# Decode attention on one core: the scores of K summed in two halves of 128 rows, the second halved three times

## Chip, cores, metric

One core of a Trainium2 chip (8 NeuronCores; the other seven idle). The metric is the device time of one launch in microseconds (us). The kernel before takes 1251.89 us (median of 3 runs, 1251.55 to 1251.96).

## The reference

Attention with one query row per head: 8 x 32 = 256 heads, 4096 keys, head size 128, bf16. K and V are 268.4 MB each and are used once.

```python
B, H, Sq, Skv, Dh = 8, 32, 1, 4096, 128
scores = jnp.einsum('bhqd,bhkd->bhqk', q, k) * q.shape[-1] ** -0.5
attn = softmax(scores, axis=-1)
return jnp.einsum('bhqk,bhkd->bhqd', attn, v)
```

## The kernel before

Eight heads make a group; there are NT = 32 groups, t = 0 to 31. A group's K is 128 partitions x C = 256 rows x D = 128. VectorE multiplies the rows by the query in place and halves the products by adding (128 -> 64, for the second half of the rows -> 32 columns). PE sums on with an identity matrix into a PSUM bank (8 partial sums for each of 64 rows), and VectorE reads the bank with a reduction. Then come the weights (VectorE, ScalarE) and a loop of 64 multiplies of PE over V. Three buffers serve all loads, in the order K(t+1), V(t), K(t+2), ...

```python
G, SLOTS = 8, 3
UC = 64;  DS = 512 // UC;  NU = C // UC
# ... (cut)
def width_of(t, u):
    return D // 4 if u >= NU // 2 and 0 < t < NT - 3 else D // 2

def product(t, lo, hi):
    kt = loads["k", t]; qb = qbs[t]; part = kt[:, lo:hi, :]
    nc.vector.tensor_tensor(out=part, in0=part, in1=qb[:].to_broadcast([P, hi - lo, D]), op=ALU.mult)
    nc.vector.tensor_tensor(out=part[:, :, 0 : D // 2], in0=part[:, :, 0 : D // 2],
                            in1=part[:, :, D // 2 : D], op=ALU.add)
    if width_of(t, lo // UC) < D // 2:
        nc.vector.tensor_tensor(out=part[:, :, 0 : D // 4], in0=part[:, :, 0 : D // 4],
                                in1=part[:, :, D // 4 : D // 2], op=ALU.add)

def sum_over_d(t, u):
    ps = ps_s.tile([P, UC, DS], F32, name="ps", tag="ps")
    n = width_of(t, u) // DS
    for s in range(n):
        nc.tensor.matmul(ps[:], lhsT=ident[:],
            rhs=kt[:, u * UC : (u + 1) * UC, s * DS : (s + 1) * DS], start=(s == 0), stop=(s == n - 1))
# ... (cut)
# one turn of the loop over t, 0 < t <= NT - 3 (cut to its order):
product(t, 0, 2 * Q); sum_over_d(t, 0); sum_over_d(t, 1)
product(t, 2 * Q, 3 * Q); sum_over_d(t, 2); scores_of(t, 0); scores_of(t, 1)
product(t, 3 * Q, C); sum_over_d(t, 3); scores_of(t, 2)
values_loop(t - 1); load("k", t + 1); load("v", t)
scores_of(t, 3); weights_of(t)
```

## Time and profile before

| quantity | before | where it is read |
|---|---|---|
| time | 1251.89 us | median of runs |
| load queue busy | 99.5% | table of DMA queues |
| VectorE busy / idle before K | 1021.9 us / 139.9 us | busy shares / waits |
| one turn of the loop | 38.7 us | timeline, first product to first product |
| V, K from issue to landing | 25.8 / 28.3 us | DMA issues |

"Busy" is the time in which an engine has at least one instruction under way. The wait that VectorE has just before the first product of a turn shows how much of the turn it does not need. The time from issue to landing, less the 19.35 us that one load of 8.39 MB takes in the steady turn (half of 38.7), shows how much of the load ahead was still to come when it was issued. I call this the **lead** of a load. A buffer is *handed over* when its last reader is done, so that the next load into it can be issued. The lines themselves are in the prediction.

### The profile page before, as it was taken

What the parts mean: (1) busy time and instruction counts of PE and PEld (TensorE: products, weight loads), DVE (VectorE), ACT (ScalarE), POOL (GpSimd) and SP (SyncE); (2) the same over time, 40 slices, a digit from 0 to 9 for tenths busy, and PEclk for the clock granted to TensorE, in tenths of its full rate; (3) what the DMA queues carried; (4) which work ended last, traced back from release to release, by engine and by line L of the source; (5) the groups of instructions that cost most, each with busy time, mean ns of one, the idle gap of its engine ahead of it and who ended that gap; (6) DMA issues with size and microseconds to landing.
All of it is one profiled execution on the core that took longest, in us unless ns stands there. A gap on an engine that the chain in (4) does not pass through costs nothing. (4 is left out here: it accounts for less than half of the span.)

```text
span 1250.2 us, 10842 instructions
## 1 busy us (share of the span) xinstructions
PE 786.8 (63%) x3116; PEld 299.6 (24%) x3116; DVE 1021.9 (82%) x495; ACT 166.1 (13%) x433; POOL 4.5 (0%) x24
## 2 busy tenths in 40 slices
PE   3366567666576655766558665577655776556755
PEld 1122123222232222322223222222222222212222
DVE  7887987878977789777798777987779877798783
ACT  0111011111011110111101111011110111101111
POOL 1000000000000000000000000000000000000000
PEclk9987788777888778877788777887778878779867
DMA  9999999999999999999999999999999999999997
GB/s 405 436 436 435 434 436 432 436 430 428 426 437 436 429 435 434 434 435 436 436 434 432 424 437 437 432 430 428 436 437 434 430 433 434 430 435 421 427 446 329
DMA packets 11432, 537.33 MB, mean 430 GB/s; under 512 B 1808, under 2 KB 2064, under 8 KB 2320
## 3 DMA queue, kind: packets, MB, share of 16 engines
q1 hardware_dynamic: 11072, 536.94, 99.5%
q8 instruction: 15, 0.25, 0.1%
q10 hardware_dynamic: 336, 0.07, 0.0%
q14 instruction: 9, 0.07, 0.0%
HBM read 536.94 MB, written 0.07 MB: 430 GB/s over the span
## 5 line engine op out<-in xcount | busy, mean ns | idle before, releaser
L191 DVE TENSOR_TENSOR kt<-kt,qb 128x8192 bf16<-128x8192 bf16 (+1 forms) x99 | 560.9, 5665 | 146.6 <-DMA kt<-in_k_dram 139.9
L211 PE MATMUL ps<-kt,ident 128*128 128x512 bf16 x800 | 278.4, 511 | 389.9 <-DVE kt L199 299.7
L294 PE MATMUL av<-vt,w 128*32 x1740 | 425.5, 397 | 4.6
L194 DVE TENSOR_TENSOR kt<-kt 128x4096 bf16<-128x4096 bf16 (+1 forms) x99 | 288.8, 2917 | 3.4
L294 PEld LDWEIGHTS av<-vt,w 128*32 x1740 | 173.4, 100 | 262.4 <-issue 119.5
L211 PEld LDWEIGHTS <-ident 128*128 128x128 bf16 x800 | 95.7, 120 | 565.4 <-issue 527.9
L223 DVE TENSOR_REDUCE sc<-ps 128x64 f32<-128x512 f32 x128 | 85.3, 685 | 54.0 <-PE ps L211 54.0
L248 ACT ACTIVATE e<-sc,nmax 128x256 bf16<-128x256 f32 x32 | 16.3, 508 | 706.7 <-DVE nmax L242 706.7
L255 ACT ACTIVATE w<-e,mine 128x256 bf16<-128x256 bf16 x256 | 105.6, 495 | 1.1
L199 DVE TENSOR_TENSOR kt<-kt 128x2048 bf16<-128x2048 bf16 x56 | 68.6, 1225 | 1.9
L351 ACT ACTIVATE comb<-av 32x512 bf16<-32x512 f32 (+1 forms) x32 | 18.8, 586 | 329.0 <-PEq L284 321.4
L280 PE MATMUL av<-vt,w 128*32 128x512 bf16 x116 | 47.2, 499 | 14.6 <-issue 13.1
L371 PE MATMUL op<-comb,pick 32*16 32x128 bf16 (+1 forms) x128 | 12.1, 213 | 20.7 <-ACT comb L351 20.7
L280 PEld LDWEIGHTS av<-vt,w 128*32 128x32 bf16 x116 | 6.9, 100 | 55.2 <-issue 55.2
L177 PE MATMUL qp<-qg,heads 8*128 8x128 bf16 x32 | 7.0, 217 | 16.7 <-ACT qg L175 16.7
L371 PEld LDWEIGHTS <-pick 32*16 32x16 bf16 (+1 forms) x128 | 8.7, 83 | 27.7 <-issue 27.3
L322 PE MATMUL av<-vt,w 128*32 128x512 bf16 x188 | 13.7, 418 | 2.3 <-DMA vt<-in_v_dram 2.3
L235 DVE TENSOR_REDUCE pmax<-sc 128x1 f32<-128x256 f32 x32 | 13.4, 420 | 1.1
L175 ACT ACTIVATE qg<-qh 8x128 bf16<-8x128 f32 x32 | 8.5, 266 | 33.5 <-PE qh L171 33.5
L171 PE MATMUL qh<-q_all,ident 128*8 128x128 bf16 x32 | 7.2, 225 | 8.7 <-DMA q_all<-in_q_dram 8.3
L179 ACT ACTIVATE qb<-qp 128x128 bf16<-128x128 f32 x32 | 8.9, 278 | 9.7 <-PE qp L177 9.7
L237 DVE TENSOR_SCALAR spread<-same,pmax 128x32 f32<-128x32 f32 x32 | 7.7, 242 | 1.1
(31 smaller groups left out, 47.7 us busy)
## 6 DMA issues: line engine op xcount, KB each, us to landing
kt<-in_k_dram SPq DMA_DIRECT2D x4, 4096.0 KB, 24.3
kt<-in_k_dram SPq DMA_DIRECT2D x4, 2048.0 KB, 13.0
vt<-in_v_dram SPq DMA_DIRECT2D x1, 4096.0 KB, 33.9
vt<-in_v_dram SPq DMA_DIRECT2D x1, 2048.0 KB, 38.5
vt<-in_v_dram SPq DMA_DIRECT2D x1, 1024.0 KB, 40.5
vt<-in_v_dram SPq DMA_DIRECT2D x1, 512.0 KB, 41.3
vt<-in_v_dram SPq DMA_DIRECT2D x31, 25.8
kt<-in_k_dram SPq DMA_DIRECT2D x29, 28.3
```

Of the source, the lines that this page charges most:

```text
L191: nc.vector.tensor_tensor(out=part, in0=part, in1=qb[:].to_broadcast([P, hi - lo, D]), op=ALU.mult)
L194: nc.vector.tensor_tensor(out=part[:, :, 0 : D // 2], in0=part[:, :, 0 : D // 2], in1=part[:, :, D // 2 : D], op=ALU.add,)
L199: nc.vector.tensor_tensor(out=part[:, :, 0 : D // 4], in0=part[:, :, 0 : D // 4], in1=part[:, :, D // 4 : D // 2], op=ALU.add,)
L211: nc.tensor.matmul(ps[:], lhsT=ident[:], rhs=kt[:, u * UC : (u + 1) * UC, s * DS : (s + 1) * DS], start=(s == 0), stop=(s == n - 1),)
L223: made = nc.vector.tensor_reduce(out=scs[t][:, u * UC : (u + 1) * UC], in_=sums.pop((t, u))[:], axis=AX.X, op=ALU.add)
L248: nc.scalar.activation(out=e[:], in_=sc[:], func=ACT.Exp, bias=nmax[:, 0:1], scale=scale, accum_out=esums[t // R][:, t % R : t % R + 1],)
L255: nc.scalar.activation(out=w[:, :, g, :], in_=e_g, func=ACT.Copy, scale=mine[:, 0, g : g + 1])
L280: pe.matmul(av, lhsT=wf[:, i * nw : (i + 1) * nw], rhs=vf[:, i * nv : (i + 1) * nv], **how)
L294: pe.matmul(av, lhsT=wf[:, bass.ds(ow + i * nw, nw)], rhs=vf[:, bass.ds(ov + i * nv, nv)], start=False, stop=False,)
L322: nc.tensor.matmul(avs[t][j * AG : (j + 1) * AG, :], lhsT=w[:, i, :, :], rhs=vt[:, c0 : c0 + CB, :], start=(i < TG), stop=(j not in group[ ...
L351: nc.scalar.activation(out=comb[0:n, :, :], in_=av[0:n, :, :], func=ACT.Copy)
L371: nc.tensor.matmul(ops[n][:], lhsT=pick[0:e, m, r, :], rhs=comb[0:e, m, :], start=(r == 0 and m == 0), stop=(r == R - 1 and m == CB - 1 an ...
```

## The change

In the loop turns the second half becomes one product over 128 rows, and each half gets one PSUM bank with four partial sums per row and one read. To keep the PE work of the second half small, it is halved three times (to 16 columns, 4 multiplies). The groups outside the loop keep quarters, and t = 29 keeps a width of 64. The intent is fewer, larger instructions on VectorE and fewer on PE.

```diff
-        return D // 4 if u >= NU // 2 and 0 < t < NT - 3 else D // 2
+        return D // 8 if lo == C // 2 and 0 < t < NT - 3 else D // 2
...
-        if width_of(t, lo // UC) < D // 2:
+        n = D
+        while n > width_of(t, lo):
+            n //= 2
             nc.vector.tensor_tensor(
-                out=part[:, :, 0 : D // 4], ...
+                out=part[:, :, 0:n], in0=part[:, :, 0:n], in1=part[:, :, n : 2 * n], op=ALU.add
             )
...
-        ps = ps_s.tile([P, UC, DS], F32, name="ps", tag="ps")
+        ps = ps_s.tile([P, BANK], F32, name="ps", tag="ps")
+        ds = BANK // (hi - lo)
...
+                sum_over_d(t, 0, HALF)
+                product(t, HALF, C)
+                sum_over_d(t, HALF, C)
+                scores_of(t, 0, HALF)
...
                 values_loop(t - 1)
                 load("k", t + 1)
                 load("v", t)
+                scores_of(t, HALF, C)
```

## The prediction

> **What bounds the kernel now.** I first read the page: the busy shares, the DMA row of the slices, and the table of DMA queues.
>
> ```profile
> PE 786.8 (63%) x3116; PEld 299.6 (24%) x3116; DVE 1021.9 (82%) x495; ACT 166.1 (13%) x433; POOL 4.5 (0%) x24
> ...
> DMA  9999999999999999999999999999999999999997
> GB/s 405 436 436 435 434 436 432 436 430 428 426 437 436 429 435 434 434 435 436 436 434 432 424 437 437 432 430 428 436 437 434 430 433 434 430 435 421 427 446 329
> ...
> q1 hardware_dynamic: 11072, 536.94, 99.5%
> ```
>
> No compute engine is full: VectorE is idle 18% of the span. The load queue is busy 99.5% of it, in every slice, at about 434 GB/s, with 536.94 MB to bring (all of K and V once). That makes the load the suspect, but a busy queue is only the bound if nothing lets it run dry, so next come the waits and one turn of the loop over t (groups of 8 heads; t = 1 to 29 take the loop form).
>
> ```profile
> DVE kt L191 <- DMA kt<-in_k_dram: 139.9, 28, 6.3
> ```
>
> The columns are us in total, times, longest. In 28 turns VectorE stands before the first product and waits for K to land: 139.9 / 28 = 5.0 us each. The timeline of one turn, VectorE and then the load issues:
>
> ```profile
> 586.22 8.69 DVE L191 TENSOR_TENSOR kt<-kt,qb 128x16384 bf16<-128x16384 bf16 x1 [4.86 <-DMA kt<-in_k_dram]
> 594.94 4.43 DVE L194 TENSOR_TENSOR kt<-kt 128x8192 bf16<-128x8192 bf16 x1
> 599.29 4.42 DVE L191 TENSOR_TENSOR kt<-kt,qb 128x8192 bf16<-128x8192 bf16 x1
> 603.74 2.29 DVE L194 TENSOR_TENSOR kt<-kt 128x4096 bf16<-128x4096 bf16 x1
> 606.07 1.22 DVE L199 TENSOR_TENSOR kt<-kt 128x2048 bf16<-128x2048 bf16 x1
> 607.21 1.28 DVE L223 TENSOR_REDUCE sc<-ps 128x64 f32<-128x512 f32 x2
> ...
> 615.24 1.22 DVE L199 TENSOR_TENSOR kt<-kt 128x2048 bf16<-128x2048 bf16 x1
> 616.38 0.68 DVE L223 TENSOR_REDUCE sc<-ps 128x64 f32<-128x512 f32 x1
> 618.41 0.69 DVE L223 TENSOR_REDUCE sc<-ps 128x64 f32<-128x512 f32 x1 [1.35 <-PE ps L211]
> ...
> 624.96 8.69 DVE L191 TENSOR_TENSOR kt<-kt,qb 128x16384 bf16<-128x16384 bf16 x1 [4.88 <-DMA kt<-in_k_dram]
> ```
>
> ```profile
> 596.57 0.33 SPq L158 DMA_DIRECT2D kt<-in_k_dram  x1
> 618.41 0.33 SPq L158 DMA_DIRECT2D vt<-in_v_dram  x1
> ```
>
> A turn lasts 624.96 - 586.22 = 38.74 us and brings two buffers of 128 x 256 x 128 x 2 bytes = 8.39 MB, so 16.78 MB / 38.74 us = 433 GB/s; one buffer takes 19.4 us. The work of VectorE, its wait for PE included, ends 4.88 us before the turn does. There are three buffers. The V load goes into the K buffer just read, so it is issued when the last summing multiply is done (618.41, which is 32.2 us after the turn's start). The K load goes into the V buffer just read, so it is issued after the loop of PE over V (596.57).
>
> ```profile
> vt<-in_v_dram SPq DMA_DIRECT2D x31, 25.8
> kt<-in_k_dram SPq DMA_DIRECT2D x29, 28.3
> ```
>
> From issue to landing, V takes 25.8 us and K 28.3, where the transfer itself takes 19.4. So when a load is issued, 6.4 us (V) or 8.9 us (K) of the load before it are still to come: the queue never runs dry, and the buffers are handed over that much earlier than needed. This margin is the number that decides the case. The chain that ended last agrees: its longest piece is 41.43 us of V loads, after which come under 2 us of PE and ScalarE.
>
> **What the Trainium skill says.** *DMA: Bandwidth & Descriptors*, section "Where 436 GB/s comes from", puts the ceiling into SBUF at 16 ports x 256 bits x 850 MHz = 435.2 GB/s. The trace agrees: 433 GB/s in a turn, 437 in the best slices. An estimate from that figure: 536.94 MB / 435.2 GB/s = 1233.8 us is a floor, 1.4% below 1251.89, which no edit of the arithmetic on K can undercut. *SBUF — State Buffer*, section "SBUF: two separate sides", says that engine ports and DMA ports don't contend. If so, less VectorE or PE work does not quicken the loads. The trace is consistent: the rate stays 430 to 434 GB/s in stretches of one turn from 300 to 1140 us although the mix of engines varies within each. *VectorE: DVE Perf Modes*, section "The perf-mode tier table", has 1224 ns for a bf16 two-tensor operation of 2048 elements (two per cycle); the trace has 1225 for the halving. It lists the reduce at one element per cycle, so its cost should follow the 512 elements read and hardly the count written. *SBUF — State Buffer*, section "Door 1: The DMA port swizzle", gives 16-byte lines, full speed needing at least two accesses to one line. The new summing multiply reads runs of 4 bf16 (8 bytes) where the old read 8 (16 bytes): still four per line. No multiply of the kernel before has such runs, so the trace can't confirm that.
>
> **The change part by part**, for t = 1 to 28 (width 16 in the second half; before it was 32):
> - First half, product and first halving: unchanged (8.69 + 4.42).
> - Second half, products: two of 4.42 become one of 8.69: -0.15 us. First halving: two of 2.29 become one of 4.42: -0.16.
> - Second halving: two of 1.225 become one over 128 x 32 = 4096 elements, which the 4096-element row gives as 2.29: -0.16. Third halving, new: 128 x 16 = 2048 elements, 1.225: +1.22.
> - Reads of PSUM: four of 0.685 become two, still 512 elements each: -1.37.
>
> VectorE: -0.15 - 0.16 - 0.16 + 1.22 - 1.37 = -0.61 us a turn, and 8 + 4 = 12 large instructions become 6 + 2 = 8. t = 29 keeps full width: -0.15 - 0.16 - 1.37 = -1.7 us, and 10 become 6. Over the kernel 28 x 0.61 + 1.7 = 19 us less: VectorE 1021.9 -> about 1003 us, 495 -> 495 - 29 x 4 = 379 instructions.
>
> PE: the first half keeps 64 / 4 = 16 multiplies (before 2 x 8), the second has 16 / 4 = 4 (before 2 x 4). Four fewer in 28 turns: 3116 - 112 = 3004 multiplies. The groups of four took 1.0 to 1.9 us in the timeline depending on the clock, so 28 x 1.45 = 41 us less: about 746 us busy. The same 512 output columns are streamed, so one multiply should cost the same.
>
> Path that hands over the K buffer: the last halving ended 30.2 us into the turn (616.46 - 586.22). Afterwards two reads (1.2 with their overlap) lie behind it instead of before it, the merged instructions save 0.5, and the third halving adds 1.15: 30.2 - 1.2 - 0.5 + 1.15 = about 29.7. Four multiplies (1.9) follow as before, so the V load is issued at +31.6 instead of +32.2, some 0.55 us earlier; the loop over V starts that much earlier, and so does the K load. But the queue has 6.4 and 8.9 us of work left at those points. An earlier issue only waits longer: V 25.8 -> about 26.4, K 28.3 -> about 28.9, and VectorE's wait for K grows from 5.0 to about 5.5 us (139.9 -> about 155 in all). On the path that sets the end: nothing. At t = 29 sixteen multiplies instead of eight follow the last halving, perhaps 3 us, partly given back by the earlier halving; this too lies within the margin. t = 0, 30 and 31 are unchanged, and the last V load still starts when the load before it ends.
>
> **Rivals.**
> 1. *VectorE is what matters, being 82% busy.* Then 19 us come off: 1251.9 - 19 = about 1233, just -1.5%, and right at the estimated floor. Against it: the 4.9 us idle before K in every turn.
> 2. *A new operation is far dearer than I take it.* The 8-byte runs might slow the multiplies, or the rows of 16 the halving. If each of the twenty multiplies took double, the four at the end add 1.9 us to the handover; the sixteen lie behind the second product (16.6 us of VectorE work). If the third halving ran at one element per cycle, +1.1. Together 3 us, less than 6.4: no change. It would take more than 4.9 us per turn on VectorE, or 6.4 in the handover, to move the time at all; 2% (25 us) needs a further 0.9 us in each of 28 turns.
> 3. *The loads run faster when the engines read less or more evenly.* Slices vary from 421 to 437 GB/s. If every slice had 436, 536.94 / 436 = 1231.5 us of loading plus some 6 us of head and tail (first issue at 0.8, landing a little after 2 us; end 2 us after the last load) is about 1238, -1.1%. Against it: within a turn the rate over 2 us windows swings with packets landing (295 to 524) and not with any engine; turns agree within 1%.
>
> **Range and chances.** The predicted time is 1251.5 us: the same loads at the same rate. Before, three runs spread over 0.4 us; the range of 1247 to 1256 allows for a slightly different rate of the queue or a start or tail shifted by a few us. Faster by over 2% means below 1226.9 us, under the estimated floor of 1233.8: 0.01. Slower by over 2% needs an operation several times dearer than its row: 0.02. Same: 0.97.
>
> **What would show it right or wrong.** Right: load queue still 99 to 100%; a turn still 38.7 us; VectorE about 1003 us and its wait for K about 155; reads of 0.69 to 0.75 us for 128x128 from 128x512; third halving 1.22; V and K landing 0.4 to 0.8 us later after issue than before. Wrong: landing times near 19.4 us (the queue ran dry), VectorE no longer waiting for K, a multiply of the sums well above 0.6 us, or turns shorter than 38.5 us, which would mean that the loads had been slowed by the engines.

## The result

The changed kernel takes 1250.93 us (median of 6 runs, 1250.80 to 1251.34), the kernel before 1251.72 us in the same rounds (1251.43 to 1252.26). The ratio is 0.9994 with a 95% interval of 0.9981 to 1.0007: the same. All ratios here are the mean time of one kernel's fast runs over that of the other's of the same rounds, so not quite the ratio of the medians quoted.

Busy shares, DMA row and load queue of the changed kernel's page:

```profile
PE 761.4 (61%) x3004; PEld 284.3 (23%) x3004; DVE 1010.6 (81%) x379; ACT 166.1 (13%) x433; POOL 4.5 (0%) x24
...
DMA  9999999999999999999999999999999999999998
...
q1 hardware_dynamic: 11072, 536.94, 99.5%
```

The instruction counts fell as intended (VectorE 495 to 379, PE 3116 to 3004), and the load queue is as full as before. One turn of VectorE (start, duration), then the issues of the loads, then the waits (us in total, times, longest) and the landing times:

```profile
586.38 8.69 DVE L189 TENSOR_TENSOR kt<-kt,qb 128x16384 bf16<-128x16384 bf16 x1 [5.21 <-DMA kt<-in_k_dram]
595.11 4.43 DVE L195 TENSOR_TENSOR kt<-kt 128x8192 bf16<-128x8192 bf16 x1
599.45 8.69 DVE L189 TENSOR_TENSOR kt<-kt,qb 128x16384 bf16<-128x16384 bf16 x1
608.17 8.02 DVE L195 TENSOR_TENSOR kt<-kt 128x8192 bf16<-128x8192 bf16 x3
616.10 0.68 DVE L219 TENSOR_REDUCE sc<-ps 128x128 f32<-128x512 f32 x1
...
618.16 0.69 DVE L219 TENSOR_REDUCE sc<-ps 128x128 f32<-128x512 f32 x1 [1.32 <-PE ps L207]
...
625.12 8.69 DVE L189 TENSOR_TENSOR kt<-kt,qb 128x16384 bf16<-128x16384 bf16 x1 [5.29 <-DMA kt<-in_k_dram]
```

```profile
596.31 0.33 SPq L156 DMA_DIRECT2D kt<-in_k_dram  x1
618.16 0.33 SPq L156 DMA_DIRECT2D vt<-in_v_dram  x1
```

```profile
DVE kt L189 <- DMA kt<-in_k_dram: 150.1, 28, 6.6
```

```profile
vt<-in_v_dram SPq DMA_DIRECT2D x31, 26.2
kt<-in_k_dram SPq DMA_DIRECT2D x29, 28.7
```

The turn is 38.74 us, as it was. The V load is issued 31.78 us into the turn instead of 32.19, and lands 26.2 us later instead of 25.8: what the engines saved, the load spent waiting behind the load ahead. Likewise VectorE's saving turned into a longer wait for K, 150.1 us against 139.9.

### The profile page after: what moved, and what is told of

Its sections match the earlier page's. It is cut to its first block, busy times and chain, and to the rows that moved or that the text cites. A ratio compares the mean times of both kernels' runs of the same rounds, so it can differ in the third digit from the quotient of the medians.

```text
span 1249.5 us, 10534 instructions
## 1 busy us (share of the span) xinstructions
PE 761.4 (61%) x3004; PEld 284.3 (23%) x3004; DVE 1010.6 (81%) x379; ACT 166.1 (13%) x433; POOL 4.5 (0%) x24
## 3 DMA queue, kind: packets, MB, share of 16 engines
q1 hardware_dynamic: 11072, 536.94, 99.5%
## 5 line engine op out<-in xcount | busy, mean ns | idle before, releaser
L189 DVE TENSOR_TENSOR kt<-kt,qb 128x16384 bf16<-128x16384 bf16 (+1 forms) x70 | 556.8, 7955 | 156.8 <-DMA kt<-in_k_dram 150.1
L207 PE MATMUL ps<-kt,ident 128*128 128x512 bf16 x688 | 253.2, 537 | 416.3 <-DVE kt L195 415.9
L195 DVE TENSOR_TENSOR kt<-kt 128x4096 bf16<-128x4096 bf16 (+1 forms) x126 | 382.7, 3037 | 4.3
L207 PEld LDWEIGHTS <-ident 128*128 128x128 bf16 x688 | 80.0, 125 | 583.0 <-DVE kt L195 444.7
L219 DVE TENSOR_REDUCE sc<-ps 128x128 f32<-128x512 f32 (+1 forms) x70 | 48.1, 687 | 57.0 <-PE ps L207 57.0
L175 PE MATMUL qp<-qg,heads 8*128 8x128 bf16 x32 | 7.0, 217 | 16.7 <-ACT qg L173 16.7
L367 PEld LDWEIGHTS <-pick 32*16 32x16 bf16 (+1 forms) x128 | 8.7, 83 | 28.9 <-issue 28.5
## 6 DMA issues: line engine op xcount, KB each, us to landing
vt<-in_v_dram SPq DMA_DIRECT2D x31, 26.2
kt<-in_k_dram SPq DMA_DIRECT2D x29, 28.7
```

The source lines that it names most:

```text
L195: nc.vector.tensor_tensor(out=part[:, :, 0:n], in0=part[:, :, 0:n], in1=part[:, :, n : 2 * n], op=ALU.add)
L207: nc.tensor.matmul(ps[:], lhsT=ident[:], rhs=kt[:, lo:hi, s * ds : (s + 1) * ds], start=(s == 0), stop=(s == n - 1),)
L219: made = nc.vector.tensor_reduce(out=scs[t][:, lo:hi], in_=ps, axis=AX.X, op=ALU.add)
L367: nc.tensor.matmul(ops[n][:], lhsT=pick[0:e, m, r, :], rhs=comb[0:e, m, :], start=(r == 0 and m == 0), stop=(r == R - 1 and m == CB - 1 an ...
```

## The experiments

**Theory:** the stream of loads sets the time; handing a buffer over earlier, or working less, only lengthens waits. **Rivals:** VectorE at 81% is the bound; busy engines slow the loads; and a question about size: how much delay of a handover the queue really hides. Twelve kernels ran; a thirteenth did not build. "Turn" in the text is, for each profile, the time from the first product of t = 2 to that of t = 29, divided by 27: 38.86 us for the kernel before, 38.82 for the changed one.

**e1: much less work.** The changed kernel without halvings and with 4 multiplies per half in the loop, arithmetically wrong. (The reference draws Q and K as normal numbers times 0.05, so the scores are tiny and the weights nearly even, and the check is all but blind to the scores.)

```diff
-        while n > width_of(t, lo):
+        while n > width_of(t, lo) and not 0 < t <= LT:
...
-        n = width_of(t, lo) // ds
+        n = 4 if 0 < t <= LT else width_of(t, lo) // ds
```

> The changed kernel with wrong results on purpose: in the loop turns VectorE does no halving at all and PE sums only 4 multiplies per half, so VectorE falls by 4.42 + 8.02 = 12.4 us a turn and the K buffer is handed over about 12 us earlier. Theory (the queue of loads is the bound, the engines don't slow it): 1249 to 1252 us, turn still 38.7 us, VectorE's wait for K about 17 us a turn, landing of V and K some 10 us later after issue. Rival 'VectorE is the bound': 29 x 12.4 = 360 us less, or the load floor of about 1234 to 1240. Rival 'busy engines slow the loads': 1236 to 1245 us with rates of 436 in the slices.

Measured: 1250.85 us, ratio 0.9994 (0.9977 to 1.0010), equal to the changed kernel.

```profile
PE 668.1 (53%) x2644; PEld 250.7 (20%) x2644; DVE 655.6 (52%) x265; ACT 166.2 (13%) x433; POOL 4.5 (0%) x24
...
vt<-in_v_dram SPq DMA_DIRECT2D x31, 38.7
kt<-in_k_dram SPq DMA_DIRECT2D x29, 40.4
```

VectorE lost 355 us of work and the time did not move. Each load now waits behind about a whole other load (38.7 us is twice 19.35). So the rival "VectorE is the bound" falls, and so does "busy engines slow the loads": the engines were far quieter, and the time was the same.

**e2, e3, e4: more work ahead of the handover.** One (e2) or two (e3) more VectorE operations of 4.42 us per turn, on columns that nobody reads any more; e4 puts the same two into the kernel before.

```diff
+    def extra(t, n):
+        dead = loads["k", t][:, 0 : C // 2, D // 2 : D]
+        for _ in range(n):
+            nc.vector.tensor_tensor(out=dead, in0=dead, in1=dead, op=ALU.add)
...
             product(t, 0, first)
+            if loop:
+                extra(t, 1)        # e2; 2 in e3 and e4
```

> The changed kernel with one more VectorE operation of 8192 elements (4.42 us) in every loop turn, after the first halving of the first half, on columns that nobody reads any more (results right). It delays both VectorE and the handover of the K buffer by 4.4 us. Theory: the wait of 5.3 us for K and the 6.8 us of margin of the V load swallow it: 1250 to 1253 us, the wait for K falls from 150 to about 25 us, V lands about 21.9 us after issue. Rival 'VectorE is the bound': +29 x 4.4 = +128 us, 1379 us.

> The same with two such operations (8.84 us a turn), which is 3.5 us more than VectorE's wait of 5.3. Theory: VectorE becomes the bound of the loop, a turn lasts 38.74 + 3.55 = 42.3 us, 28 turns x 3.55 = about +100 us, 1345 to 1360 us, the load queue runs dry for a few us in each turn. Rival 'VectorE is the bound already': +256 us, 1507 us. If the margin were much larger than read from the trace: 1251 us.

> The kernel before with the same two operations. Theory: with VectorE as the bound the change's saving on it, 0.37 us a turn as read from the two traces (31.83 against 32.20), should come out: 28 x 0.37 = 10 us more than the changed kernel with the same two operations, so about 1362 us against 1351 (0.8%). Rival 'the change saves nothing that counts even there' : both equal within 2 us. By the sum of my prediction (0.61 us a turn): 17 us apart.

Measured: e2 1284.13 us (1.0255), e3 1356.19 us (1.0830), e4 1364.85 us (1.0904); turns 40.01, 42.27 and 42.67. e3 is as expected: in it VectorE no longer waits for K and a turn is as long as its work. In that regime the change's saving comes out, 8.7 us (0.40 us a turn, expected 0.37). But **e2 missed**: it should have cost nothing, and cost 33 us. In this stretch its turns alternate; first the V issues, then the first products of the turns:

```profile
561.47 0.33 SPq L156 DMA_DIRECT2D vt<-in_v_dram  x1
...
600.18 0.33 SPq L156 DMA_DIRECT2D vt<-in_v_dram  x1
...
641.79 0.33 SPq L156 DMA_DIRECT2D vt<-in_v_dram  x1
```

```profile
563.95 8.69 DVE L189 TENSOR_TENSOR kt<-kt,qb 128x16384 bf16<-128x16384 bf16 x1 [0.81 <-DMA kt<-in_k_dram]
...
605.55 8.69 DVE L189 TENSOR_TENSOR kt<-kt,qb 128x16384 bf16<-128x16384 bf16 x1 [3.71 <-DMA kt<-in_k_dram]
...
644.73 8.69 DVE L189 TENSOR_TENSOR kt<-kt,qb 128x16384 bf16<-128x16384 bf16 x1 [1.27 <-DMA kt<-in_k_dram]
```

VectorE still waits for K in every turn, so it is not the bound. The V load of 561.47 is issued 563.95 - 561.47 = 2.5 us before the K ahead of it has landed, and the turn that follows takes 605.55 - 563.95 = 41.6 us. The next has a lead of 605.55 - 600.18 = 5.4 us, and its turn takes 39.2. The load queue's share fell from 99.5% to 97.8%. So a lead of 2.5 us is too short: part of the queue runs dry before the last byte of the load ahead has landed. The traffic around the two issues shows it, in stretches of 2.42 us, the time of one row of 64 KB (columns: the stretch and its length, VectorE busy, granted clock, DMA share, GB/s):

```profile
557.62:560.04 2.42, 2.39 (x4) 0.50 0.38 163
560.04:562.46 2.42, 1.06 (x4) 0.50 0.47 162
562.46:564.88 2.42, 1.54 (x4) 0.68 0.80 271
...
600.42:602.84 2.42, 1.33 (x4) 0.77 1.02 433
```

In the trace's packet records 13 of the 16 DMA engines had finished their part of K by 560.4 us and the last one at 563.5, and the first packet of V started at 562.4, about 1.0 us after its issue. In between most of the engines had nothing to do. Idle engines make up about 22 of the 35 us by which the profiled span grew (2.2% of 1285.0 us, less 0.5% of 1249.5); in the other 13 or so the packets themselves took longer, mostly the first ones after such a gap (3.0 to 3.6 us instead of 2.42 for most of those at 562.4).

**f1, g1: the same work after the handover.** To part VectorE's idle time from the handover. f1 needed a scratch tile for which there was no room, and did not build.

> Run e2 fell short of what I expected (1284 us, not 1251): either VectorE needs its idle time before K, or the later handover of the K buffer is what cost 33 us. Here the changed kernel gets four VectorE operations of 2048 elements (4 x 1.2 = about 4.7 us) at the end of each loop turn, after the handover, on a scratch tile: as much VectorE work as e2, but the loads are issued as in the changed kernel. If the handover cost it: 1250 to 1252 us, VectorE's wait for K down to about 0.6 us a turn, V and K landing 26.2 and 28.7 us after issue as in the changed kernel. If VectorE's idle time was needed: about 1284 us as e2.

g1 does it with eleven more reductions of the scores into an unused number, behind the weights:

```diff
         ws[t] = w
+        if 0 < t <= LT:
+            junk = small.tile([P, 1], F32, name="junk", tag="junk")
+            for _ in range(11):
+                nc.vector.tensor_reduce(out=junk[:], in_=sc[:], axis=AX.X, op=ALU.max)
```

> What f1 should have been (its scratch tile found no room; here 11 more reductions of the scores into one unused number, 11 x 0.42 less overlap = about 4.4 us a turn of VectorE after the handover, results right). If the later handover is what cost e2 its 33 us: 1250 to 1252 us, VectorE's wait for K about 0.9 us a turn, landing times as in the changed kernel (26.2 and 28.7). If VectorE needs its idle time: about 1284 us as e2.

Measured: 1253.91 us, ratio 1.0020 (1.0003 to 1.0037), turn 38.92. From its page and its waits:

```profile
PE 765.8 (61%) x3004; PEld 285.2 (23%) x3004; DVE 1141.0 (91%) x698; ACT 166.1 (13%) x433; POOL 4.5 (0%) x24
```

```profile
DVE kt L189 <- DMA kt<-in_k_dram: 17.0, 27, 1.6
```

VectorE is as busy as in e2 (1141.0 us; e2 has 1138.9) and waits 0.6 us a turn, less than the 2.0 us of e2, yet costs 3 us, not 33. It is the late handover that costs, not the work. The 3 us, outside my 1250 to 1252, are not explained: in the profile the last V load lands 2.4 us later than in the changed kernel, though the leads are as there. With 0.6 us left any late landing may reach VectorE, but I did not test that.

**f2: half the delay.** `C // 4` in place of `C // 2` in `extra`, 2.29 us.

> As e2 but with half the extra work ahead of the handover (4096 elements, 2.29 us a turn). In e2 the V load was issued 2.5 us before the K load ahead of it landed in full, and the queue ran dry; the loss of 1.1 us a turn puts the knee at about 3.6 to 5.3 us. Here it is issued 7.0 - 2.3 = 4.7 us before. If the margin behaves so: 1250 to 1262 us, V landing about 24 us after issue. If each us of delay costs time from the first on: about 1268 us (half of e2).

Measured: 1256.68 us (1254.25 to 1258.42), ratio 1.0045; V lands 24.0 us after issue, a lead of 24.0 - 19.35 = 4.65 us; turn 38.88. The loss is not in proportion to the delay: 2.29 us cost 6 us, 4.42 us cost 33. Nor is it clear that the 6 us are a matter of the queue. Here is the loop from 80 to 1130 us in f2 and then in e2, and the first line of the chain that ended last in f2 and then in the changed kernel:

```profile
80.00:1130.00 1050.00, 922.00 (x337) 0.79 1.00 433
80.00:1130.00 1050.00, 951.84 (x329) 0.79 0.98 420
```

```profile
DVE 3%; PE 1%; ACT 0%; issue 0%; ACTq 0%; DVEq 0%
DMA 3%; DVE 1%; PE 1%; SPq 0%; issue 0%; ACT 0%; DVEq 0%
```

In f2's loop the load queue is as full as in the changed kernel (also 1.00 and 433 GB/s). Of the 3.0 us by which its profiled span is longer, the last V load lands 1.6 us later, and 1.4 us come after it: VectorE starts group 30 at 1166.75 us instead of 1163.85, never waits for data again, and the end is set by VectorE, ScalarE and PE, where in the changed kernel the last V loads set it. The profile is of the fastest of the four runs (1254.25 us); where the others lost 2 to 4 us more is not known.

**g3, g4: only the V buffer later.** 12 and 24 more multiplies ahead of each loop over V, overwritten at once:

```diff
         with tc.tile_critical() as loop:
+            for _ in range(12):        # 24 in g4
+                one(0, start=True, stop=True)
             for i in range(EDGE):
```

> The changed kernel with 12 more multiplies ahead of each loop over V (overwritten at once, results right), 12 x 0.253 = 3.0 us; only the handover of the V buffer, so the K load, comes later. K is issued 9.35 us before the load ahead of it lands; 6.3 would be left, above the knee of about 4 us seen in e2 and f2: 1250 to 1252 us, K landing 25.7 us after issue.

> The same with 24 more multiplies, 6.1 us: 3.3 us left before the load ahead lands, between f2 (4.7 us left, 0.17 us a turn lost) and e2 (2.5 left, 1.14 lost). By that knee about 0.7 us a turn lost: 1260 to 1280 us. If the margin is the full 9.35 us as my prediction read it from the landing times: 1251 us.

Measured: g3 1251.25 us (0.9998), K lands 27.3 us after issue; g4 1254.83 us (1.0024), K lands 24.7 us after issue. The delays were smaller than planned (1.4 and 4.0 us, from the landing times against 28.7), because the extra multiplies take up the stretch of slow clock with which the loop starts (in the changed kernel 0.50 at 618.5 to 621 us and 1.00 from 624): its 60 multiplies took 14.8 us in the changed kernel and 13.1 here. The leads are therefore 7.95 us (nothing lost) and 5.35 us (4 us lost over the kernel, turn 38.88). My forecast for g4 was too dear since its lead was not the 3.3 us assumed. Its 4 us show no lack of lead either: as in f2, the DMA share of the loop is 1.00 at 433 GB/s, and the chain that ended last runs through VectorE, ScalarE and PE. Of the 3.2 us in the profiled span 2.0 come after the last landing.

**What lead the queue needs.** Where the queue falls idle can be counted from the packet records around each issue. In e2 the V loads with a lead under 3 us cost 0.4 to 2.6 us of idle engines each (mean of all 16), those from 3 to 4.6 us up to 0.8, and those of 4.9 us or more at most 0.1. In f2, with leads around 4.5 us counted one by one, hardly any: 0.5 us in all its turns. So the queue here begins to lose time somewhere between 3 and 4.5 us, and not at 6.4.

**h1: e2 with an earlier handover.** V loads cut into two halves of rows, in three fixed buffers whose halves are tracked apart, so that the first half of the K buffer is handed over early. VectorE has e2's work.

```diff
-        buf = kv_pool.tile([P, C, D], BF16, name=f"{kind}t", tag="kv")
+        if len(loads) < SLOTS:
+            fixed.append(kv_pool.tile([P, C, D], BF16, name=f"kv{len(loads)}", tag=f"kv{len(loads)}"))
+        buf = fixed[len(loads) % SLOTS]
...
-        for n in cuts.get((kind, t), [C]):
+        for n in cuts.get((kind, t), [C // 2] * 2 if kind == "v" else [C]):
```

> Run e2 again (4.42 us more of VectorE work ahead of the handover), but each V load is cut into two halves of rows, into three fixed buffers whose halves are tracked on their own: the half of the K buffer that was summed first can be overwritten some 13 us before the other. VectorE is as busy as in e2 and the late half is issued as late. If e2's 33 us came from V loads issued too late for the queue to stay full: 1250 to 1256 us, VectorE's wait for K down to 0.5 to 1 us a turn. If they came from VectorE itself or from the sheer busy share: about 1284 us as e2.

Measured: 1300.59 us and a **wrong result** (relative error 0.175), so the total says nothing about the question. The cause of both is an edit of mine: at t = 30 the load of V(30) is written down ahead of the product that reads K(30) out of the same buffer. A rotating buffer sorts that out; a fixed one takes the written order, and the product waits for V. The waits of h1 show it as one wait of 49.8 us for V. If the output of one group of 32 is lost, the error should be about sqrt(1/32) = 0.177. The loop turns before it are not touched by that and can be read:

```profile
587.08 8.69 DVE L192 TENSOR_TENSOR kv<-kv,qb 128x16384 bf16<-128x16384 bf16 x1 [0.93 <-DMA kv<-in_k_dram]
...
625.78 8.69 DVE L192 TENSOR_TENSOR kv<-kv,qb 128x16384 bf16<-128x16384 bf16 x1 [0.80 <-DMA kv<-in_k_dram]
```

The turn is 38.89 us on average, against 40.01 in e2 and 38.82 in the changed kernel: with the handover mended, e2's work is hidden again, with 0.8 to 1.0 us of VectorE to spare. What stays open is the time of a correct kernel of this form, and how far the fixed buffers alone matter.

**g2: the merge without the third halving.** `D // 8` becomes `D // 4`.

> The changed kernel with the second half halved only twice (width 32, so 8 summing multiplies instead of 4 behind it): the merging of the instructions alone. VectorE 28 x 1.15 to 1.22 = 32 to 34 us less busy than the changed kernel (about 977), the handover 1.2 us earlier by VectorE and up to 1.9 later by PE. Time by the load theory: 1250 to 1252 us. If the change had gained anything through its smaller work on PE, this would be slower than the changed kernel by a few us.

Measured: 1250.79 us, ratio 0.9994; VectorE 976.3 us busy, PE 789.5. Merging alone, or merging with the third halving, gives the same time: 34 us less of VectorE, 28 us more of PE, nothing on the clock.

**f3, f4: half the bytes.** From t = 2 each load brings half its buffer (fixed buffers, as in h1; wrong data), in the changed kernel (f3) and in the one before (f4).

```diff
+            m = n // 2 if len(loads) >= SLOTS and (kind, t) not in cuts else n
-            dma = nc.sync.dma_start(buf[:, c0 : c0 + n, :], src[t, :, c0 : c0 + n, :])
+            dma = nc.sync.dma_start(buf[:, c0 : c0 + m, :], src[t, :, c0 : c0 + m, :])
```

> The changed kernel with wrong data on purpose: from t = 2 on each load brings only the first half of its buffer (three fixed buffers, the rest keeps old data), the last loads excepted; 8.39 MB a turn. Theory (loads are the bound): the loads take 19.4 us a turn, VectorE with about 33.5 us becomes the bound, 28 turns x 5.2 us less: about 1105 us. If something other than loads paced the turn: near 1250 us.

> The kernel before with the same half loads. Theory: VectorE paces it at 33.86 us a turn, 28 x 0.37 = about 10 us above the changed kernel of the same rounds, as e4 stood 8.7 us above e3. If the change saves VectorE nothing: equal within 2 us.

Measured: 1139.71 us (0.9105) and 1156.45 us (0.9229), both wrong. With half the load the time falls at once, which no cut of work achieved. The turns are 33.33 us (f3) and 34.10 (f4). The totals carry the same slip at t = 30 as h1 (one wait of 48.1 us for V in f3), which is why f3 lies above the 1105 expected; f4 stands 16.7 us above f3 where 10 were expected. The loop alone gives 27 x (38.82 - 33.33) = 148 us less. Freed from the loads, the change is worth 0.77 us a turn, more than VectorE's 0.37: in f4 VectorE also waits for PE in the middle of some turns (47 waits for PE of 59.2 us in all, against 32 of 51.2 us in f3), which the changed order avoids:

```profile
574.07 0.68 DVE L227 TENSOR_REDUCE sc<-ps 128x64 f32<-128x512 f32 x1
575.39 0.69 DVE L227 TENSOR_REDUCE sc<-ps 128x64 f32<-128x512 f32 x1 [0.64 <-PE ps L215]
```

Apart from these two with half the bytes, no version that ran is faster than the changed kernel by more than its spread.

## Why the prediction was right

*The bound.* Right. Predicted 1251.5 us, measured 1250.93. It rested on the full load queue and the wait for K; e1 (355 us of VectorE work removed, same time) and f3 (half the bytes, 148 us off the loop) show both sides of it.

*The parts.* The third halving took 1.225 us and the read of 128x128 from 128x512 took 0.688, as taken. VectorE fell by 11.3 us instead of 19 (1010.6 measured, 1003 predicted). The term at fault is the adding of mean durations: per turn they give -0.61 us, the union of the intervals in the windows of one turn gives 31.83 - 32.20 = -0.37. In the turn shown, a VectorE record whose input doesn't come from the one in front often starts about 0.08 us before the other ends (before the change, the second product starts at 599.29 and the halving in front ends at 599.37). Such overlaps were free already. The trace has six of them in this turn before and three after, and three at 0.08 us make the 0.24 missing. PE fell by 25 us instead of 41: the group that went is the one in the middle of the turn, and it took 1.02 us in most turns (the median), at a granted clock of 1.00 in the turn shown. I had taken 1.45 us, a mean that includes the group at the end of the turn, which stays (1.86 us at 0.50). 28 x 1.02 = 29 us is near what came.

*Readings.* All the sums come out as written. One reading was loose: the GB/s row that the prediction shows has a slice of 446, and 405 and 329 at its ends, so 437 is not its highest and 421 not its lowest.

*The handover.* Predicted +31.6 us and 0.55 us earlier, measured +31.78 and 0.41 us earlier. Landing 26.2 and 28.7 us after issue (predicted 26.4 and 28.9), waits for K 150.1 us (predicted 155).

*The margin.* Here a size was wrong without harm. I read 6.4 us (V) and 8.9 us (K) as free to be used up, since a load of 19.4 us landed that much later than it would alone. By e2 and f2 the queue begins to lose time when the lead falls to somewhere between 4.5 and 3 us (2.5 us: about 3 us lost in that one turn; 4.5 us: next to nothing). So of V's 6.45 us about 2, and at most 3.5, are free. Had the change delayed VectorE and the handover by 4.4 us, my rule in rival 2 (under 4.9 us on VectorE and under 6.4 in the handover: no change) would have predicted "same" where e2 shows 2.6%. That the error did no harm is luck of the direction: this change hands over earlier.

*The rivals.* VectorE as the bound: refuted by e1. Dearer operations: not seen. With the 8-byte runs four multiplies at the end of the turn took 1.89 us after 1.86 before, at a granted clock of 0.50 both times, and the sixteen of the first half 5.32 after 5.30 (medians). Quieter engines and faster loads: refuted by e1. The 0.7 to 0.8 us by which the changed kernel, e1 and g2 stand below the one before lies inside the interval, and I leave it open.

## What to carry to other kernels

Where one queue of loads is busy 99% of the span, ask first of a change when it hands buffers over. Read the lead of each load (time to landing less the time of one load), and count only what lies above the lead that the queue needs to stay full, here between 3 and 4.5 us and not zero. An engine that waits for data in every turn could take on nearly that much more work here behind the handover (g1, 3 us lost); the same work ahead of it cost ten times as much (e2). And look at the end of the kernel apart from the loop: a delay that the loop hides may come out there (f2, g4).

## What the Trainium skill lacked or had wrong

- *DMA: Bandwidth & Descriptors*: the section on queues, rings and completion order does not say how early a load must be issued behind another on the same queue for the engines to stay busy. For loads of 8.39 MB in 64 KB rows the runs show that between 3 and 4.5 us ahead of the landing of the load in front are needed; at 2.5 us a turn lost about 3 us.
